# Zero products in the first softmax chain, running sums of squares over 73 tiles, and a sixth output buffer, in a fused attention and highway kernel

## The chip, the cores and the metric

The kernel runs on one core of a Trainium2 chip. The metric is the device time of one launch in microseconds (us), the median of several executions. The profile's span is counted from the first instruction and is 1.7 to 1.9 us shorter than the times. The engines are PE (TensorE, matrix products), DVE (VectorE), ACT (ScalarE), POOL (GpSimd, which here also issues the loads) and SP (SyncE, which issues the stores). The "granted clock" is the share of PE's full clock that the trace shows. In the trace of the kernel before it is full for 27.31 us from 14.29 on, half for 3.41 and full again for 228.69, which is 8, 1 and 67 times 3.41 us; pieces of that length, counted from where a trace's clock record starts, are called throttle windows here. The "issue" of a product is the time from its start to the next start when nothing is waited for.

## The reference

```python
# q, k, v: 4 batches x 6336 x 256 f32
qn = q / (np.linalg.norm(q, axis=1, keepdims=True) + 1e-06)
kn = k / (np.linalg.norm(k, axis=1, keepdims=True) + 1e-06)
s = kn.transpose(0, 2, 1) @ qn / tau          # 256 x 256 per batch
a = softmax(s, -1)
x = v @ a                                      # 6336 x 256 per batch
H = relu(x @ w_h); T = sigmoid(x @ w_t + b_t)  # highway layer
out = T * H + (1 - T) * x
```

Each batch has a reduction over all its rows (k'q and the norms), then a small chain of dependent steps (norms, softmax, transpose, products with the weights), and only then its outputs.

## The kernel before

Rows are cut into tiles of 128. Phase 1 of a batch takes one tile after another ("p1 tile"); the k'q product goes to `S`, the squared norms are the diagonals of k'k and q'q in `G`:

```python
for c in range(2):
    kc = kk[0:nr, bass.ts(c, P)]
    nc.tensor.matmul(S[:, c, :], kc, qq[0:nr, :], ...)      # 128x256
    nc.tensor.matmul(G[:, c, :], kc, kc, ...)               # 128x128
for c in range(2 if squared(b, j) is None else 0):
    qc = qq[0:nr, bass.ts(c, P)]
    nc.tensor.matmul(G[:, 2 + c, :], qc, qc, ...)           # 128x128
```

For some tiles ("squared" ones) ACT squares q and DVE adds the squares up, so PE is spared the last two products. A product with ones ("sums") then folds the sum over the partitions.

Outputs are made in 100 slots of two tiles. PE transposes v (`vt_bank`, four transposes to a slot, called a set here; DVE copies it to `vts`), then does three products: `zbank` (the gate, ACT takes the sigmoid to `tt`), `h` and `x`. DVE makes `th` and `ux`, POOL subtracts them into an output tile `o`. Between the slots of batch b, PE does the p1 tiles of batch b+1:

```python
for t in range(NSLOT):
    ...                                   # transposes of v, zbank, h, x
    pending.append((t, *products(t, h, x)))           # DVE: th, ux
    ...
    for _ in range(count):                            # p1 tiles of the next batch
        p1_tile(pb + 1, j); squares(pb + 1, j); done1 += 1
    if t not in (end1 - 1, end1):
        next_loads(2, now)                            # POOL issues loads
    room = DEFER - sum(t >= at for at in DRAIN)       # stores held back
    out_now = 0
    while len(stores) > room and out_now < 2:
        note(send_store(last), now); out_now += 1     # SP: 1 MB, four slots
```

So up to DEFER finished stores are kept waiting while loads are urgent, and at each slot listed in DRAIN one fewer is kept. How the transposes run ahead of the slots is a table (`TURNS`: at slot 61 two, at slot 68 none), and where each step of a chain goes is another.

Of the kernel before, what the change touches and what calls it, by code (L numbers as in the profile page):

```python
# [15 lines left out]
P = 128  # L16
# [3 lines left out]
def kernel(  # L20
# [41 lines left out]
    QFIRST = [QALL.index((b, 0)) for b in range(B)]  # L62
    QTILES = 8
    QRING = 6
    ORING = 5
    DEFER = 3
    DRAIN = [53, 74, 85]
    VG = [spans(6, 10, 12, 12, 9)] + [spans(12, 12, 12, 13)] * (B - 1)
    VTILES = 13
    VALL = [(b, g) for b in range(B) for g in range(len(VG[b]))]  # L70
# [1 line left out]
    VRING = 4  # L72
    NPAIR = (NS + 1) // 2
    LOOK = 3
    RAMP = 14
    REM_SLOT = 4
    START_US = 5

    CHAIN0 = (0, 0, 1, 2)
    HEAD = sum(CHAIN0)  # L80
    P1_END = [18, 42, 64]

    GATES = {9: 2, 24: 0, 28: 2, 57: 2, 60: 2, 61: 2, 62: 0, 68: 0, 70: 0, 73: 0, 95: 2}
    TURNS = {29: 0, 30: 2, 48: 1, 49: 2, 55: 2, 57: 2, 61: 2, 68: 0, 74: 0, 75: 0, 76: 0, 93: 2}
    VTS = 9
    TTS = 6

    PE_BIAS = (67, 70, 72, 74, 77)

    DVE_SUBS = (98, 99)  # L90

# [1 line left out]



    SQ_GROUPS = {1: (1, 4), 2: (2, 3, 4), 3: (3, 4)}
    SQ_TILES = 8
    SQ_CUTS = 4
    LULL = [0, 3, 1, 5]

    EARLY = {"sums": (0, "pre"), "norms": (0, "pre"), "invs": (2, "pre"), "cq": (2, "pe"), "logits": (3, "pre"), "exps": (3, "post"), "softmax": (4, "pre"), "at": (4, "pe"), "at_copy": (5, "pre"), "ahat": (5, "pe"), "ahat_copy": (6, "pre")}
    LAST = {"sums": (0, "pre"), "norms": (0, "pre"), "invs": (1, "pre"), "cq": (2, "pe"), "logits": (2, "post"), "exps": (4, "post"), "softmax": (4, "post"), "at": (6, "pe"), "at_copy": (8, "pre"), "ahat": (8, "pe"), "ahat_copy": (9, "pre")}
    PLACES = [None, EARLY, EARLY, LAST]

    ctx.enter_context(tc.manual_schedule())
    const_pool = ctx.enter_context(tc.tile_pool(name="consts", bufs=1))
# [44 lines left out]
    for n in range(QRING):  # L151
        load_q(n)
        load_k(n)
    bt_sb = const_pool.tile([65, C], f32, tag="bt")
    nc.vector.memset(bt_sb, 0.0)
    for r in (0, 32, 64):
        nc.sync.dma_start(out=bt_sb[r : r + 1, :], in_=moe_b_t.rearrange("(a m) -> a m", a=1))
# [19 lines left out]
    zeros = const_pool.tile([P, 2 * C], f16, tag="zeros")  # L177
    nc.vector.memset(zeros.bitcast(u16), 0)

    rem0 = const_pool.tile([P, 2, C], f16, tag="rem0")  # L180
    nc.vector.tensor_copy(out=rem0[0:REM, :, :], in_=rem0_32[0:REM, :, :])
    wht = const_pool.tile([P, 2, 2 * C], f16, tag="wht")

# [43 lines left out]
                used.add(("q", QFIRST[b] + g))  # L227


    sq_t, part_t, sum_t = {}, {}, {}  # L230
    cuts = []

    def squared(b, j):

        for n, g in enumerate(SQ_GROUPS.get(b, ())):
            s0, ns = QG[b][g]
            o = j - (s0 + ns - SQ_TILES)
            if 0 <= o < SQ_TILES:
                return n, g, o
        return None  # L240

    def squares(b, j):

        at = squared(b, j)
        if at is None or at[2] % 2 == 0:
            return
        n, g, o = at
        if o == 1:
            add_up(len(cuts) - SQ_CUTS)

            sq_t[b] = work_pool.tile(
                [P, SQ_TILES // 2, C, 2], f32, tag="sq", bufs=2, name=f"sq{b}_{n}"
            )
            if n == 0:
                count = len(SQ_GROUPS[b])
                part_t[b] = work_pool.tile(
                    [P, (count + 1) // 2, C, 2], f32, tag="sq_part", bufs=1, name=f"part{b}"
                )
                if count % 2:
                    nc.vector.memset(part_t[b][:, count // 2, :, 1], 0.0)  # L260
        q0 = j - 1 - QG[b][g][0]
        nc.scalar.activation(  # L262
            out=sq_t[b][:, o // 2, :, :].rearrange("p c u -> p u c"),
            in_=q_t[QFIRST[b] + g][:, q0 : q0 + 2, :], func=Act.Square,
        )
        if o == SQ_TILES - 1:
            sq, part = sq_t[b], part_t[b]
            for i in range(SQ_CUTS):
                cols = slice(i * C // SQ_CUTS, (i + 1) * C // SQ_CUTS)
                cuts.append((  # L270
                    part[:, n // 2, cols, n % 2],
                    sq[:, :, cols, :].rearrange("p m c u -> p c m u"),
                ))
            if n == len(SQ_GROUPS[b]) - 1:
                sum_t[b] = work_pool.tile([P, C], f32, tag="sq_sum", bufs=1, name=f"sum{b}")
                cuts.append((sum_t[b], part.rearrange("p m c u -> p c m u")))

    def add_up(k):
        while k > 0 and cuts:
            dst, source = cuts.pop(0)  # L280
            nc.vector.tensor_reduce(  # L281
                out=dst, in_=source, op=AluOp.add, axis=mybir.AxisListType.XY
            )
            k -= 1
# [4 lines left out]
    def chain(b):  # L289
# [105 lines left out]
        def exps():  # L395

            ar = st["ar"] = st["t1"]
            rs = st["rs"] = small("rs", [P, 2], bufs=2)
            for c in range(2):
                nc.scalar.activation(  # L400
                    out=ar[:, c, :], in_=st["t1"][:, c, :], func=Act.Exp,
                    scale=st["inv"][:, c : c + 1], accum_out=rs[:, c : c + 1],
                )
            if b == 0:
                preload_table(Act.Sigmoid)

                st["e16"] = small("e16", [P, 2, C], f16)
                for c in range(2):
                    nc.vector.tensor_copy(out=st["e16"][:, c, :], in_=ar[:, c, :])

# [301 lines left out]

    ones_hl = const_pool.tile([65, P], f16, tag="ones_hl")
    bt_hl = const_pool.tile([65, C], f16, tag="bt_hl")
    bt_r = const_pool.tile([65, C], f32, tag="bt_r")

    def bias_rows():
        nc.vector.memset(ones_hl.bitcast(u16), 0)
# [62 lines left out]
    next_loads(3, now)  # L781
    c0 = chain(0)

    def fill(n):
        nonlocal done1
        for _ in range(n):
            p1_tile(1, done1)
            done1 += 1

    c0["norms"]()  # L790
    c0["invs"]()
    fill(CHAIN0[0])
    c0["cq"]()
    c0["logits"]()
    turns = [(t, transpose(t)) for t in range(2)]
    fill(CHAIN0[1])
    c0["exps"]()
    c0["at"]()
    fill(CHAIN0[2])
# [21 lines left out]
    for t in range(NSLOT):  # L821
        b, i = divmod(t, NPAIR)
        ready = set(used)
        slot[0] = t
        run(t, "pre")
        zs = range(zdone, min(NSLOT, zdone + GATES.get(t, 1)))
        zdone = zs.stop
        turned = range(tdone, min(NSLOT, tdone + TURNS.get(t, 1)))
        tdone = turned.stop
        for s in zs:  # L830
            mains(s, zbank[s % 2], 2, True)
            gate_act(s, zbank[s % 2])
        if pending:
            last = subtract(*pending.pop())
        for s in turned[:1]:
            vt_copy(s, transpose(s))
        for s in zs:
            seed(s, zbank[s % 2])
        h = hx_tile(f"h{t}")
        mains(t, h, 1, False)  # L840
        x = hx_tile(f"x{t}")
        mains(t, x, 0, False)
        for s in turned[1:]:
            vt_copy(s, transpose(s))
        run(t, "pe")
        pending.append((t, *products(t, h, x)))
        add_up(2 if len(cuts) > SQ_CUTS else 1)
        run(t, "post")
        for s in turned:
            bb, ii = divmod(s, NPAIR)  # L850
            for g, (s0, ns) in enumerate(VG[bb]):
                if 2 * ii + 2 == s0 + ns or (g == len(VG[bb]) - 1 and ii == NPAIR - 1):
                    used.add(("v", VFIRST[bb] + g))
        if t == NSLOT - 1:
            last = subtract(*pending.pop())


        pb = done1 // (NS + 1)
        count = 0
        for s in turned:  # L860
            bb, ii = divmod(s, NPAIR)
            g = max(g for g in range(len(VG[bb])) if VG[bb][g][0] <= 2 * ii)
            now = max(now, landed.get((load_v, VFIRST[bb] + g), now))
        now += 1.5
        if pb < len(P1_END):
            left = P1_END[pb] - t
            if 0 <= t - end1 < len(LULL):
                due = LULL[t - end1]
            else:
                due = -(-((pb + 1) * (NS + 1) - done1) // left)  # L870
            for ahead in range(due):
                if left > 1 and tile_lands(done1 + ahead) > now + 0.43 * ahead:
                    break
                count += 1
        for _ in range(count):
            pb, j = divmod(done1, NS + 1)
            now = max(now, min(tile_lands(done1), now + 20.0)) + 0.43
            p1_tile(pb + 1, j)
            squares(pb + 1, j)
            done1 += 1  # L880
            if j == NS:
                end1 = t + 1
                steps = chain(pb + 1)
                for name, (at, when) in PLACES[pb + 1].items():
                    hooks.setdefault((t + 1 + at, when), []).append(steps[name])


        if t not in (end1 - 1, end1):
            next_loads(2, now)
        room = DEFER - sum(t >= at for at in DRAIN)  # L890
        out_now = 0
        while len(stores) > room and out_now < 2:
            note(send_store(last), now)
            out_now += 1
        vT_t.pop(t, None)
# [38 lines left out]
```

## Time and profile before

| | before |
|---|---|
| time, median | 279.58 us |
| span of the profile | 278.1 us |
| PE busy | 255.7 us (92%) |
| DVE busy | 200.5 us (72%) |
| HBM read / written | 78.4 MB / 26.0 MB |

PE's busy time is the first thing to read, but an average hides the stages: PE follows the loads up to 37.5 us, runs into the first chain until 48, and is then full to 266. The lines of these views stand in the prediction. A pair of numbers that the page does not give, the time at which a load landed, and the time at which PE first used it, I took from the trace, by pairing each load with the first product on its tiles. The execution that was traced took 279.9 us, a little more than the median. Holes of PE in the text are counted from the time at which it could have issued its next product; the views count them from the modelled end of the product before, which makes them about 0.16 us shorter (four zbank products that take 0.44 us of issue are shown as 0.60).

### The profile page before, as it was taken

How to read it: one execution, taken by the hardware profiler on the slowest of the kernel's cores; microseconds unless marked ns; L12 is line 12 of the kernel's file. 1: busy time of each engine (PE TensorE's matmuls, PEld its weight loads, DVE VectorE, ACT ScalarE, POOL GpSimd, SP SyncE). 2: the span in 40 equal slices, each digit the busy share in tenths (PEclk: the TensorE clock that was granted, in tenths of full speed). 3: DMA queues.
4: the chain of work that ended last, by engine and by line, in shares of the span. 5: the costliest groups of instructions: out<-in, count | busy, mean ns of one | idle time of the engine just before them, and what ended most of it. 6: DMA issues, size and time to landing. Idle time of an engine off the chain costs nothing.

```text
span 278.1 us, 6881 instructions
## 1 busy us (share of the span) xinstructions
PE 255.7 (92%) x2772; PEld 226.1 (81%) x2772; DVE 200.5 (72%) x436; ACT 159.1 (57%) x277; POOL 171.9 (62%) x191
## 2 busy tenths in 40 slices
PE   0689859999999899999999999999999999999990
PEld 0579757999999788899999988899998887999870
DVE  0060046994666885779999865678989999999993
ACT  1040055687264469588854677477753775777660
POOL 6232350899565393764689857464545797888780
PEclk9999997999999999999999999999999999999996
DMA  6999999999999999999999999999999877837353
GB/s 125 213 214 214 209 209 210 213 214 214 214 216 213 285 216 286 213 287 302 273 240 262 235 272 271 233 297 320 315 224 251 262 140 298 341 151 305 154 226 105
DMA packets 16726, 65.65 MB, mean 236 GB/s; under 512 B 1843, under 2 KB 4150, under 8 KB 13750
## 3 DMA queue, kind: packets, MB, share of 16 engines
q0 software_dynamic: 11744, 39.13, 71.1%
q1 hardware_dynamic: 4950, 26.09, 23.7%
q8 instruction: 21, 0.34, 0.5%
q14 instruction: 11, 0.09, 0.1%
HBM read 78.38 MB, written 25.95 MB: 375 GB/s over the span
## 4 chain that ended last, share of the span: by engine, by line
PE 81%; DMA 10%; DVE 5%; issue 1%; ACT 1%; POOL 0%; DVEq 0%; ACTq 0%; POOLq 0%
PE zbank L552 15%; PE h L552 15%; PE x L552 15%; PE S L217 13%; DMA k<-in_k_dram 10%; PE vt_bank L525 8%; PE G L220 6%; PE G L223 4%; PE ah L445 2%; DVE ux L625 1%; DVE th L620 1%; DVE vts L538 1%; PE sums L303 1%; DVE part L281 0%; ACT ssb L400 0%
## 5 line engine op out<-in xcount | busy, mean ns | idle before, releaser
L635 POOL TENSOR_TENSOR o<-th,ux 128x512 f32<-128x512 f32 x95 | 120.9, 1279 | 33.7 <-DVE ux L625 30.9
L552 PEld LDWEIGHTS <-vts 128*128 128x128 f16 x1200 | 109.7, 98 | 15.0 <-issue 4.2
L604 ACT ACTIVATE tt<-zbank 128x512 f32<-128x512 f32 x100 | 58.9, 596 | 63.5 <-PE zbank L552 56.4
L217 PE MATMUL S<-q,k 128*128 128x256 f16 x392 | 84.4, 278 | 10.3 <-DMA k<-in_k_dram 10.3
L220 PE MATMUL G<-k 128*128 128x128 f16 x392 | 75.2, 223 | 0.0
L620 DVE SCALAR_TENSOR_TENSOR th<-h,tt 128x512 f32<-128x512 f32 (+1 forms) x104 | 69.1, 667 | 5.4 <-PE h L552 1.0
L625 DVE SCALAR_TENSOR_TENSOR ux<-tt,x 128x512 f32<-128x512 f32 (+1 forms) x104 | 68.1, 657 | 0.0
L538 DVE COPY vts<-vt_bank 128x512 f16<-128x512 f16 x96 | 40.4, 421 | 29.0 <-PE vt_bank L525 28.8
L552 PE MATMUL x<-mr,vts 128*128 128x256 f16 (+1 forms) x400 | 60.5, 273 | 0.1
L552 PE MATMUL h<-mr,vts 128*128 128x256 f16 (+1 forms) x400 | 60.6, 273 | 0.0
L552 PE MATMUL zbank<-mr,vts 128*128 128x256 f16 (+1 forms) x400 | 59.5, 273 | 0.0
L608 ACT COPY zbank<-btb 128x512 f32<-128x512 f32 x93 | 54.5, 591 | 2.6
L217 PEld LDWEIGHTS <-k 128*128 128x128 f16 x392 | 39.1, 100 | 14.7 <-DMA k<-in_k_dram 10.7
L220 PEld LDWEIGHTS <-k 128*128 128x128 f16 x392 | 39.1, 100 | 0.9
L223 PE MATMUL G<-q 128*128 128x128 f16 x280 | 39.5, 224 | 0.0
L525 PE MATMUL vt_bank<-ident,v 128*128 128x128 f16 x392 | 38.1, 219 | 0.6 <-DVE vts L538 0.4
L525 PEld LDWEIGHTS <-v 128*128 128x128 f16 x392 | 29.8, 98 | 4.1 <-issue 1.9
L123 POOL DMA_DIRECT2D q<-in_q_dram x28 | 15.8, 563 | 20.8 <-DMA q<-in_q_dram 7.0
L129 POOL DMA_DIRECT2D k<-in_k_dram x28 | 15.3, 546 | 21.5 <-DMA k<-in_k_dram 10.4
L223 PEld LDWEIGHTS <-q 128*128 128x128 f16 x280 | 22.2, 100 | 2.0
L281 DVE TENSOR_REDUCE part<-sq 128x64 f32<-128x512 f32 x28 | 18.7, 682 | 0.0
L262 ACT ACTIVATE sq<-q 128x512 f32<-128x512 f16 x28 | 18.5, 674 | 0.0
(99 smaller groups left out, 112.3 us busy)
## 6 DMA issues: line engine op xcount, KB each, us to landing
out_dram<-o SPq DMA_DIRECT2D x23, 1024.0 KB, 9.0
q<-in_q_dram POOLq DMA_DIRECT2D x20, 512.0 KB, 18.4
k<-in_k_dram POOLq DMA_DIRECT2D x20, 512.0 KB, 19.9
v<-in_v_dram POOLq DMA_DIRECT2D x11, 768.0 KB, 22.0
v<-in_v_dram POOLq DMA_DIRECT2D x3, 832.0 KB, 28.0
out_dram<-o SPq DMA_DIRECT2D x4, 256.0 KB, 2.0
q<-in_q_dram POOLq DMA_DIRECT2D x3, 320.0 KB, 18.1
k<-in_k_dram POOLq DMA_DIRECT2D x3, 320.0 KB, 17.2
```

The lines of the kernel that those rows point to most:

```text
L217: nc.tensor.matmul(S[:, c, :], kc, qq[0:nr, :], start=first and c == 0, stop=last and c == 1)
L220: nc.tensor.matmul(G[:, c, :], kc, kc, start=first and c == 0, stop=False)
L223: nc.tensor.matmul(G[:, 2 + c, :], qc, qc, start=False, stop=last and c == 1)
L281: nc.vector.tensor_reduce(out=dst, in_=source, op=AluOp.add, axis=mybir.AxisListType.XY)
L525: nc.tensor.transpose(ps[:, u, c, 0 : nr[u]], vt[0 : nr[u], bass.ts(c, P)], ident[0 : nr[u], 0 : nr[u]],)
L538: nc.vector.tensor_copy(out=sb, in_=ps)
L552: nc.tensor.matmul(dst[0:r, u, :], vT_t[t][:, u, kt, 0:r], mr[:, part, kt, :], start=(not seeded and kt == 0 and (u == 0 or i == NPAIR - 1 ...
L604: nc.scalar.activation(out=tt_t[s], in_=z, func=Act.Sigmoid)
L608: nc.scalar.copy(out=z, in_=btb)
L620: nc.vector.scalar_tensor_tensor(out=th[pr, us, :], in0=h[pr, us, :], scalar=0.0, in1=tt[pr, us, :], op0=AluOp.max, op1=AluOp.mult,)
L625: nc.vector.scalar_tensor_tensor(out=ux[pr, us, :], in0=tt[pr, us, :], scalar=1.0, in1=x[pr, us, :], op0=AluOp.subtract, op1=AluOp.mult,)
L635: last = eng.tensor_tensor(out=ot[pr, o0 + us.start : o0 + us.stop, :], in0=th[pr, us, :], in1=ux[pr, us, :], op=AluOp.subtract,)
```

## The change

The intent: keep PE's clock up in the first chain with products of zeros; let ACT and DVE square 73 tiles instead of 56, in runs that need not follow the load groups, with the sum carried from one run into the next instead of being kept in parts; and hold one more store back, which takes a sixth output buffer. The tables of placements are retuned with it. Its core:

```diff
-    ORING = 5
-    DEFER = 3
-    DRAIN = [53, 74, 85]
+    ORING = 6
+    DEFER = 4
+    DRAIN = [56, 75, 72, 79]
+    WARM = (14, 9)
-    CHAIN0 = (0, 0, 1, 2)
+    CHAIN0 = (0, 0, 0, 4)
-    TURNS = {29: 0, 30: 2, 48: 1, 49: 2, 55: 2, 57: 2, 61: 2, 68: 0, 74: 0, 75: 0, 76: 0, 93: 2}
+    TURNS = {49: 2, 51: 1, 52: 2, 59: 1, 61: 2, 64: 0, 72: 0, 73: 0, 93: 2}
-    SQ_GROUPS = {1: (1, 4), 2: (2, 3, 4), 3: (3, 4)}
+    SQ_RUNS = {1: (6, 14, 21, 28), 2: (17, 26, 35), 3: (13, 22, 32)}
...
+        for i in range(SQ_CUTS):
+            cuts.append((
+                sq_t[b][:, SQ_TILES // 2 - 1, cols, 1] if more else sum_t[b][:, cols],
+                sq[:, :, cols, :].rearrange("p m c u -> p c m u"),
+            ))
...
+    def keep_warm(n):
+        bank = hx_tile("warm")
+        for i in range(n):
+            nc.tensor.matmul(bank[:, i % 2, :], zeros[:, 0:P], zeros[:, 0:C], ...)
...
     c0["invs"]()
+    keep_warm(WARM[0])
...
     fill(CHAIN0[1])
+    keep_warm(WARM[1])
     c0["exps"]()
```

Cut: the tables of gates, bias slots and chain steps, the constants by which loads and p1 tiles are spread over the slots, the code of the runs, and some constants that moved into shared buffers to make room.

More of the change, by code (lines that the diff above doesn't have):

```diff
@@ L74 @@
     LOOK = 3
-    RAMP = 14
-    REM_SLOT = 4
-    START_US = 5
-    CHAIN0 = (0, 0, 1, 2)
+    RAMP = 11
+    REM_SLOT = 3
+    START_US = 4
+    WARM = (14, 9)
+    CHAIN0 = (0, 0, 0, 4)
     HEAD = sum(CHAIN0)
     P1_END = [18, 42, 64]
-    GATES = {9: 2, 24: 0, 28: 2, 57: 2, 60: 2, 61: 2, 62: 0, 68: 0, 70: 0, 73: 0, 95: 2}
-    TURNS = {29: 0, 30: 2, 48: 1, 49: 2, 55: 2, 57: 2, 61: 2, 68: 0, 74: 0, 75: 0, 76: 0, 93: 2}
+    GATES = {14: 2, 20: 0, 24: 2, 51: 2, 54: 2, 55: 2, 58: 0, 67: 0, 69: 0, 73: 0, 95: 2}
+    TURNS = {49: 2, 51: 1, 52: 2, 59: 1, 61: 2, 64: 0, 72: 0, 73: 0, 93: 2}
     VTS = 9
     TTS = 6
-    PE_BIAS = (67, 70, 72, 74, 77)
+    PE_BIAS = (71, 72, 76, 79, 97)
     DVE_SUBS = (98, 99)
     V_HELD = {}
-    SQ_GROUPS = {1: (1, 4), 2: (2, 3, 4), 3: (3, 4)}
+    SQ_RUNS = {1: (6, 14, 21, 28), 2: (17, 26, 35), 3: (13, 22, 32)}
     SQ_TILES = 8
     SQ_CUTS = 4
-    LULL = [0, 3, 1, 5]
-    EARLY = {"sums": (0, "pre"), "norms": (0, "pre"), "invs": (2, "pre"), "cq": (2, "pe"), "logits": (3, "pre"), "exps": (3, "post"), "softmax": (4, "pre"), "at": (4, "pe"), "at_copy": (5, "pre"), "ahat": (5, "pe"), "ahat_copy": (6, "pre")}
-    LAST = {"sums": (0, "pre"), "norms": (0, "pre"), "invs": (1, "pre"), "cq": (2, "pe"), "logits": (2, "post"), "exps": (4, "post"), "softmax": (4, "post"), "at": (6, "pe"), "at_copy": (8, "pre"), "ahat": (8, "pe"), "ahat_copy": (9, "pre")}
-    PLACES = [None, EARLY, EARLY, LAST]
+    SQ_RATE = 2
+    LULL = [2, 3, 0, 4]
+    EARLY = {"sums": (0, "pre"), "norms": (0, "pre"), "invs": (1, "pre"), "cq": (1, "pe"), "logits": (2, "pre"), "exps": (2, "post"), "softmax": (4, "pre"), "at": (4, "pe"), "at_copy": (5, "pre"), "ahat": (5, "pe"), "ahat_copy": (6, "pre")}
+    MID = {"sums": (0, "pre"), "norms": (0, "pre"), "invs": (2, "pre"), "cq": (2, "pe"), "logits": (2, "post"), "exps": (3, "post"), "softmax": (3, "post"), "at": (5, "pe"), "at_copy": (6, "pre"), "ahat": (6, "pe"), "ahat_copy": (7, "pre")}
+    LAST = {"sums": (0, "pre"), "norms": (0, "pre"), "invs": (2, "pre"), "cq": (2, "pe"), "logits": (2, "post"), "exps": (3, "pre"), "softmax": (5, "post"), "at": (7, "pe"), "at_copy": (8, "pre"), "ahat": (8, "pe"), "ahat_copy": (9, "pre")}
+    PLACES = [None, EARLY, MID, LAST]
     ctx.enter_context(tc.manual_schedule())
@@ L153 @@
         load_k(n)
-    bt_sb = const_pool.tile([65, C], f32, tag="bt")
+    bt_sb = work_pool.tile([P, 2, C], f32, tag="ux", bufs=4, name="bt_sb")[0:65, 0, :]
     nc.vector.memset(bt_sb, 0.0)
@@ L178 @@
     nc.vector.memset(zeros.bitcast(u16), 0)
-    rem0 = const_pool.tile([P, 2, C], f16, tag="rem0")
+    rem0 = work_pool.tile([P, 2, 2, P], f16, tag="vTs", bufs=VTS, name="rem0").rearrange(
+        "p u c r -> p u (c r)"
+    )
     nc.vector.tensor_copy(out=rem0[0:REM, :, :], in_=rem0_32[0:REM, :, :])
@@ L227, in p1_tile, with q_tiles @@
                 used.add(("q", QFIRST[b] + g))
-    sq_t, part_t, sum_t = {}, {}, {}
+    sq_t, sum_t = {}, {}
     cuts = []
     def squared(b, j):
-        for n, g in enumerate(SQ_GROUPS.get(b, ())):
-            s0, ns = QG[b][g]
-            o = j - (s0 + ns - SQ_TILES)
-            if 0 <= o < SQ_TILES:
-                return n, g, o
-        return None
+        for n, j0 in enumerate(SQ_RUNS.get(b, ())):
+            count = SQ_TILES - (n > 0)
+            if j0 <= j < j0 + count:
+                return n, j - j0, count
+        return None
+    def q_tiles(b, j, count):
+        g = max(i for i in range(len(QG[b])) if QG[b][i][0] <= j)
+        o = j - QG[b][g][0]
+        return q_t[QFIRST[b] + g][:, o : min(o + count, QG[b][g][1]), :]
     def squares(b, j):
         at = squared(b, j)
-        if at is None or at[2] % 2 == 0:
+        if at is None:
             return
-        n, g, o = at
-        if o == 1:
-            add_up(len(cuts) - SQ_CUTS)
+        n, o, count = at
+        if o == 0 and n == 0:
             sq_t[b] = work_pool.tile(
@@ L253, in squares @@
             )
-            if n == 0:
-                count = len(SQ_GROUPS[b])
-                part_t[b] = work_pool.tile(
-                    [P, (count + 1) // 2, C, 2], f32, tag="sq_part", bufs=1, name=f"part{b}"
-                )
-                if count % 2:
-                    nc.vector.memset(part_t[b][:, count // 2, :, 1], 0.0)
-        q0 = j - 1 - QG[b][g][0]
-        nc.scalar.activation(
-            out=sq_t[b][:, o // 2, :, :].rearrange("p c u -> p u c"),
-            in_=q_t[QFIRST[b] + g][:, q0 : q0 + 2, :], func=Act.Square,
-        )
-        if o == SQ_TILES - 1:
-            sq, part = sq_t[b], part_t[b]
-            for i in range(SQ_CUTS):
-                cols = slice(i * C // SQ_CUTS, (i + 1) * C // SQ_CUTS)
-                cuts.append((
-                    part[:, n // 2, cols, n % 2],
-                    sq[:, :, cols, :].rearrange("p m c u -> p c m u"),
-                ))
-            if n == len(SQ_GROUPS[b]) - 1:
-                sum_t[b] = work_pool.tile([P, C], f32, tag="sq_sum", bufs=1, name=f"sum{b}")
-                cuts.append((sum_t[b], part.rearrange("p m c u -> p c m u")))
+        sq = sq_t[b]
+        if o % 2 == 0 and o < count - 1:
+            return
+        first = o - o % 2
+        while first <= o:
+            src = q_tiles(b, j - o + first, o + 1 - first)
+            u = first % 2
+            nc.scalar.activation(
+                out=sq[:, o // 2, :, u : u + src.shape[1]].rearrange("p c u -> p u c"),
+                in_=src, func=Act.Square,
+            )
+            first += src.shape[1]
+        if o < count - 1:
+            return
+        add_up(len(cuts))
+        more = n < len(SQ_RUNS[b]) - 1
+        if more:
+            sq_t[b] = work_pool.tile(
+                [P, SQ_TILES // 2, C, 2], f32, tag="sq", bufs=2, name=f"sq{b}_{n + 1}"
+            )
+        else:
+            sum_t[b] = work_pool.tile([P, C], f32, tag="sq_sum", bufs=1, name=f"sum{b}")
+        for i in range(SQ_CUTS):
+            cols = slice(i * C // SQ_CUTS, (i + 1) * C // SQ_CUTS)
+            cuts.append((
+                sq_t[b][:, SQ_TILES // 2 - 1, cols, 1] if more else sum_t[b][:, cols],
+                sq[:, :, cols, :].rearrange("p m c u -> p c m u"),
+            ))
     def add_up(k):
@@ L405, in exps @@
                 preload_table(Act.Sigmoid)
-                st["e16"] = small("e16", [P, 2, C], f16)
+                st["e16"] = work_pool.tile(
+                    [P, 2, 2, P], f16, tag="vTs", bufs=VTS, name="e16"
+                ).rearrange("p u c r -> p u (c r)")
                 for c in range(2):
@@ L714 @@
     bt_hl = const_pool.tile([65, C], f16, tag="bt_hl")
-    bt_r = const_pool.tile([65, C], f32, tag="bt_r")
+    bt_r = work_pool.tile([P, 2, C], f32, tag="ux", bufs=4, name="bt_r")[0:65, 0, :]
     def bias_rows():
@@ L782 @@
     c0 = chain(0)
+    def keep_warm(n):
+        bank = hx_tile("warm")
+        for i in range(n):
+            nc.tensor.matmul(
+                bank[:, i % 2, :], zeros[:, 0:P], zeros[:, 0:C], start=True, stop=True,
+                skip_group_check=True,
+            )
     def fill(n):
@@ L846 @@
         pending.append((t, *products(t, h, x)))
-        add_up(2 if len(cuts) > SQ_CUTS else 1)
+        add_up(2 if len(cuts) > SQ_RATE else 1)
         run(t, "post")
```

## The prediction

> **What bounds the kernel now.** I read first which engine is busy in each stage, then what that engine waits for, then its clock, then the order of instructions in the one stage where it is not busy. The stretches (busy time of each engine, then granted clock, DMA share, GB/s):
>
> ```profile
> core 0: us, PE busy (x) PEld busy (x) DVE busy (x) ACT busy (x) POOL busy (x), PEclk, DMA share, GB/s
> 9.50:37.50 28.00, 26.10 (x304) 23.00 (x302) 4.63 (x22) 3.37 (x7) 8.07 (x16) 1.00 1.09 211
> 37.50:48.00 10.50, 7.02 (x60) 5.53 (x61) 6.75 (x28) 6.66 (x15) 2.77 (x5) 0.84 1.13 212
> 48.00:92.00 44.00, 44.00 (x507) 40.57 (x505) 32.07 (x59) 26.13 (x45) 32.82 (x38) 1.00 1.06 218
> 92.00:154.00 62.00, 61.26 (x682) 54.66 (x679) 52.67 (x108) 41.86 (x72) 40.88 (x46) 1.00 1.05 261
> 154.00:213.00 59.00, 58.99 (x664) 52.75 (x662) 45.75 (x97) 38.33 (x67) 35.73 (x36) 1.00 1.04 269
> 213.00:266.00 53.00, 52.76 (x528) 45.75 (x526) 51.04 (x111) 38.88 (x68) 42.22 (x37) 1.00 0.67 231
> ```
>
> Up to 37.5 us PE follows the loads of batch 0. From 37.5 to 48 (the first softmax chain) it is busy 7.02 of 10.5 us, at a mean clock of 0.84. From 48 to 266 PE has no holes but two: 0.74 us after 92 and 0.24 in the last stretch. So time there falls only if PE gets less to do, or nothing at all happens. DVE is close behind from 213 on (51.04 of 53). The DMA engines are full up to about 203 us, but PE does not wait for them after 37.5, as its list of waits shows (total, times, longest):
>
> ```profile
> PE S L217 <- DMA k<-in_k_dram: 10.3, 2, 9.2
> PE cq L372 <- DVE dcat L350: 1.7, 1, 1.7
> PE at L435 <- DVE e L409: 1.3, 2, 1.1
> ...
> PE sums L303 <- DVE sum L281: 0.7, 1, 0.7
> ```
>
> The two data waits of L217 are in the load stage. The wait for "sums" is the hole after 92: the last tile of batch 1 ends at about 94.0, DVE still adds up squares (two reductions and the sum over partial sums), and the product starts at 94.78.
>
> The clock, in pieces of one throttle window (the trace's granted clock falls to half at 41.60 and comes back at 45.01, 3.41 us later):
>
> ```profile
> 26.60:30.00 3.40, 2.34 (x33) 2.05 (x31) 0.00 (x0) 0.00 (x0) 0.71 (x1) 1.00 1.06 210
> 34.80:38.20 3.40, 2.70 (x37) 2.39 (x34) 0.66 (x7) 0.70 (x2) 1.70 (x4) 1.00 1.23 201
> 38.20:41.60 3.40, 1.30 (x14) 1.09 (x14) 2.37 (x14) 2.88 (x9) 2.00 (x4) 1.00 1.12 220
> 41.60:45.00 3.40, 3.22 (x20) 2.37 (x19) 2.12 (x7) 2.00 (x4) 0.14 (x1) 0.50 1.05 216
> ```
>
> The window with PE busy 1.30 of 3.40 us (38%) is followed by one at half clock. Windows with 2.34 (69%) and 2.70 (79%) are not. In the slow one lie the transposes of the attention matrix, one tile of batch 1 and the "ah" products, that is the chain itself:
>
> ```profile
> 41.95 0.40 PE L435 MATMUL at<-ident,e 128*128 128x128 f16 x2 [0.18 <-DVE e L409]
> 42.14 0.42 PE L217 MATMUL S<-q,k 128*128 128x256 f16 x1
> 42.38 0.42 DVE L441 COPY at_sb<-at 128x512 f16<-128x512 f16 x1 [0.49 <-PE at L435]
> 42.99 1.92 PE L445 MATMUL ah<-wht,at_sb 128*128 128x256 f16 x8
> 44.94 0.47 ACT L468 ACTIVATE mr<-ah,rinv 128x256 f16<-128x256 f32 x1 [0.38 <-PE ah L445]
> 45.45 0.48 DVE L470 TENSOR_SCALAR mr<-ah,rinv 128x256 f16<-128x256 f32 x1 [0.78 <-ACT mr L468]
> 45.85 0.41 DVE L538 COPY vts<-vt_bank 128x512 f16<-128x512 f16 x1
> 46.32 0.38 PE L525 MATMUL vt_bank<-ident,v 128*128 128x128 f16 x4 [0.42 <-DVE vts L538]
> ...
> 48.75 0.60 PE L552 MATMUL zbank<-mr,vts 128*128 128x256 f16 x4
> ```
>
> PE's next work after its tiles (the transposes at 46.32) waits for a DVE copy, which waits for a DVE scaling, which waits for ScalarE, which waits for the slow "ah" products.
>
> [...] 3.41 us at half clock, and 0.21 us instead of 0.109 from one 256-column matmul to the next. [...] the median step of G<-q here is 56 ns. [...] the trace has 682 ns for 512 elements (60 ns less when the next follows at once, as 0.60 us steps show). [...] here PE is already full after 48 us, so only the first 48 us and PE's own work have anything to give.
>
> **The change part by part.**
>
> *Zero products.* 14 products (128x256) go after the first norms, 9 after the first transposes of v. At 0.109 us: 14 x 0.109 = 1.53 us, from 37.4 to 38.9, and the chain's cq starts at 39.21; 9 x 0.109 = 0.98 us, from about 40.2 to 41.2, and the transposes start at 41.46. Both fit into the holes with 0.25 us to spare. They take a bank of the three-bank ring each time, and by the order of allocation none is awaited. The window from 38.2 gets 0.7 + 0.98 us more, so 1.30 becomes 3.0 of 3.40 (88%), above the 69% that kept the clock. I take it that the clock stays full.
>
> *What that and the new order give in the chain.* One tile of batch 1 stood before "ah", two behind it and a fourth in slot 0; now four stand behind. The copy of the transposed matrix ends 0.1 us sooner (42.7); "ah" takes 8 x 0.109 = 0.87, to 43.6; four tiles at 0.44 (36.01 to 36.45, from one to the next) end at 45.4. The other branch: last "ah" result about 43.8, ScalarE to 44.4, DVE to 44.9, copy to 45.3, so it no longer holds PE. The transposes start at 45.4 instead of 46.32. From them to the zbank product of slot 1 it was 48.75 - 46.32 = 2.43 us, less the tile that has moved (0.44) 1.99, so that product starts at 47.4: **1.35 us** gained.
>
> *Squares.* 73 tiles instead of 56 (29 instead of 16 in batch 1, 22 for 24 in batch 2, 22 for 16 in batch 3). Each takes two 128x128 products from PE: 17 x 2 x 0.056 = **1.9 us**, all where PE is full. ScalarE gets 31 pairs and 11 single tiles for 28 pairs: 3 x 0.674 + 11 x about 0.48 (like the 128x256 exponentials, 0.50) = +7.3 us, of 63.5 that it idles before tt. DVE gets 40 reductions of 0.682 for 28 plus three sums and a memset: 27.3 for 22.0, +5.3 us. Batch 1 is densest: six squared tiles a slot, so PE 1.53 + 6 x 0.33 = 3.5 us, ScalarE about 1.15 + 3 x 0.64 = 3.1, DVE 1.53 + 2.4 = 3.9 in two slots that flush four reductions and 2.7 in the next. DVE falls back 0.9 us and recovers, with two slots of copies in hand. I count nothing for it.
>
> *The sum carried along.* The partial sums and their last reduction (0.69) go. Behind the last tile of batch 1 DVE has two reductions (1.2 us) instead of two and the sum (1.9). The hole before "sums" shrinks from 0.8 to 0.15: **0.65 us**.
>
> *Sixth buffer, later drains.* A store waits for a fifth finished group instead of a fourth, so at least 1 MB of stores, at 2.5 us each (the step between 1 MB loads, as 70.3, 72.8, 75.4 us), is behind the loads until slot 72. No wait is removed by it today; it makes room for the faster PE.
>
> *Rest.* Five bias products by PE stay five; one moves to slot 97, in the tail, where it replaces a ScalarE copy that PE waited 0.13 us for. Pace in the tail stays 1.53 us a slot: zero.
>
> Sum: 1.35 + 1.9 + 0.65 = 3.9 us, so 275.7. Two tenths of small stalls make it **275.8 us** (-1.35%).
>
> **The rivals.**
>
> *The loads become the bound.* Against landing times, first uses have 4 to 6 us to spare in batch 1, but 3.8 for the sixth group of batch 2, 0.9 for the sixth of batch 3 (landed 196.5, used 197.4) and 0.8 for the last v group of batch 2 (206.7, 207.5). PE comes there about 3.7 us sooner. One deferred store gives 2.5, two (between slots 53 and 56) give 5. So the wait would be 3.7 - 0.9 - 2.5 = 0.3 us at worst by this sum. If stores were not what delays these loads, it would be 2.8 us, and the time 278.5. The 90% and more of DMA share to 203 us speaks against that[...].
>
> *The clock drops in spite of the zeros* [...]. Then 0.85 us of "ah" and the cold tiles come back, some 1.2 us: 277.0. For it: the idle gap around the copy at 42.4 remains. Against it: 69% was enough.
>
> *DVE or ScalarE becomes the bound* in batch 1 or in the chain of batch 3 (DVE 96% there). Half of the 1.9 us would be lost: 276.8. Against it: at 213 on, DVE has one reduction of 0.6 in place of the sum's 0.69, nothing more.
>
> *Much more than predicted.* PE has only 1.0 us of holes after 48 us, so beyond 4.3 us nothing is left: 275.3. 2% would be 274.0.
>
> **Range and chances.** Centre 275.8; the upper side takes one rival of about 1.3 us, the lower side the holes: 274.9 to 277.3. Faster by over 2% needs 5.6 us, more than PE's holes and removed work hold: 0.03. Slower by over 2% needs several rivals at once: 0.01.
>
> **What would show it.** Right: granted clock 1.0 through the first chain, "ah" pace 0.109, the zbank product of slot 1 near 47.4; G<-q down from 280 to 246; the wait of "sums" gone; PE full from 48 us on, last PE work about 4 us sooner; the tail from slot 64 as long as before. Wrong: a half-clock window before 48 us; PE waits for k, q or v after 160 us; PE waits for vts or tt between slots 11 and 18; a longer last stretch.

The paces were read from the trace of the kernel before: 0.109 us from one 256-column product to the next, 0.056 from one 128-column product to the next, 0.682 for one reduction.

## The result, and the profile after

The changed kernel took 277.56 us (276.77 to 277.79, 4 runs) against 279.54 for the kernel before in the same rounds. The ratio is 0.9925 (95% interval 0.9902 to 0.9947). Such a ratio is the mean time of one kernel's fast runs over that of the other's of the same rounds, so it is not quite the ratio of the quoted medians. The prediction said 275.8, with a range from 274.9 to 277.3: the direction was right, the gain was 2.0 us instead of 3.7, and the time lies outside the range.

The stretches of the changed kernel, columns as before (busy time and instructions of PE, PEld, DVE, ACT, POOL; granted clock; DMA share; GB/s):

```profile
core 0: us, PE busy (x) PEld busy (x) DVE busy (x) ACT busy (x) POOL busy (x), PEclk, DMA share, GB/s
37.50:48.00 10.50, 9.49 (x101) 7.83 (x98) 7.61 (x30) 7.09 (x15) 2.88 (x5) 1.00 1.15 213
154.00:213.00 59.00, 57.63 (x638) 51.33 (x636) 46.54 (x97) 40.54 (x73) 35.27 (x36) 1.00 1.05 272
213.00:266.00 53.00, 52.60 (x528) 45.74 (x527) 51.60 (x105) 38.57 (x68) 42.83 (x37) 1.00 0.69 240
```

The first chain is what was forecast: the clock is 1.00 and PE is busy 9.49 us of 10.5, the zeros included. But 154 to 213, which had 58.99 of 59 before, now has 57.63. PE's waits (total, times, longest; lines cut) name it:

```profile
PE vt_bank L543 <- DMA v<-in_v_dram: 1.4, 1, 1.4
...
PE cq L393 <- ACT dcat L374: 0.3, 1, 0.3
PE x L570 <- DVE th L638: 0.3, 1, 0.3
```

A wait of 1.4 us for a load of v is new; so are 0.3 us before the last chain's cq and 0.3 us before one x. In order of time, around slot 61 of the changed kernel (start, duration, engine, line):

```profile
204.25 0.60 PE L570 MATMUL zbank<-mr,vts 128*128 128x256 f16 x4
206.21 0.40 PE L543 MATMUL vt_bank<-ident,v 128*128 128x128 f16 x4 [1.36 <-DMA v<-in_v_dram]
206.44 0.38 PE L570 MATMUL h<-mr,vts 128*128 128x256 f16 x2
```

Four zbank products take 0.44 us of issue, so the transposes could have begun at 204.69; they began at 206.21, 1.52 us later, when the last v group of batch 2 had landed. The chain that ended last, in order of time, therefore runs through that load for 31.78 us:

```profile
174.38 31.78 DMA v<-in_v_dram
```

Where the gain stood at each slot (start of the slot's first h product, us):

| | before | changed | gained so far |
|---|---|---|---|
| slot 1 | 49.41 | 48.04 | 1.37 |
| slot 18 (batch 1 summed) | 95.88 | 92.28 | 3.60 |
| slot 42 (batch 2 summed) | 155.27 | 152.31 | 2.96 |
| slot 61 | 206.65 | 202.26 | 4.39 |
| slot 62 | 208.85 | 206.44 | 2.41 |
| slot 64 (batch 3 summed) | 214.56 | 211.71 | 2.85 |
| slot 94 | 262.63 | 260.43 | 2.20 |
| end of the span | 278.1 | 276.0 | 2.1 |

So the gain had been made, and was given back: at slot 61 to 62, and again between 64 and 94. (The smaller fall from slot 18 to 42 is a hole of 0.4 us at 130.7, and two squared tiles fewer than before in batch 2.)

The work that was to move did move. The groups of the page, PE's q'q products (280 before) and ACT's squares (28 before):

```profile
L230 PE MATMUL G<-q 128*128 128x128 f16 x246 | 34.2, 221 | 0.0
...
L272 ACT ACTIVATE sq<-q 128x512 f32<-128x512 f16 (+1 forms) x42 | 23.8, 606 | 0.0
```

### The profile page after: what moved, and what is told of

Its sections match the earlier page's. It is cut to its first block, busy times and chain, and to the rows that moved or that the text cites. A ratio compares the mean times of both kernels' runs of the same rounds, so it can differ in the third digit from the quotient of the medians.

```text
span 276.0 us, 6880 instructions
## 1 busy us (share of the span) xinstructions
PE 254.0 (92%) x2761; PEld 224.9 (81%) x2761; DVE 204.4 (74%) x444; ACT 164.3 (60%) x291; POOL 172.0 (62%) x191
## 4 chain that ended last, share of the span: by engine, by line
PE 69%; DMA 21%; DVE 5%; issue 1%; ACT 1%; POOL 1%; DVEq 0%; ACTq 0%; POOLq 0%
PE x L570 13%; PE h L570 13%; PE zbank L570 13%; DMA v<-in_v_dram 12%; PE S L224 11%; DMA k<-in_k_dram 10%; PE vt_bank L543 7%; PE G L227 5%; PE G L230 3%; PE ah L463 1%; DVE ux L643 1%; DVE th L638 1%; DVE vts L556 1%; PE sums L319 1%; PE cq L393 1%
## 5 line engine op out<-in xcount | busy, mean ns | idle before, releaser
L224 PE MATMUL S<-q,k 128*128 128x256 f16 x392 | 81.8, 276 | 10.4 <-DMA k<-in_k_dram 10.4
L227 PE MATMUL G<-k 128*128 128x128 f16 x392 | 73.6, 221 | 0.0
L230 PE MATMUL G<-q 128*128 128x128 f16 x246 | 34.2, 221 | 0.0
L272 ACT ACTIVATE sq<-q 128x512 f32<-128x512 f16 (+1 forms) x42 | 23.8, 606 | 0.0
L230 PEld LDWEIGHTS <-q 128*128 128x128 f16 x246 | 19.3, 99 | 1.6
L297 DVE TENSOR_REDUCE sq<-sq 128x64 f32<-128x512 f32 x28 | 18.0, 677 | 0.0
```

Source lines behind the costliest of these rows:

```text
L224: nc.tensor.matmul(S[:, c, :], kc, qq[0:nr, :], start=first and c == 0, stop=last and c == 1)
L227: nc.tensor.matmul(G[:, c, :], kc, kc, start=first and c == 0, stop=False)
L230: nc.tensor.matmul(G[:, 2 + c, :], qc, qc, start=False, stop=last and c == 1)
L272: nc.scalar.activation(out=sq[:, o // 2, :, u : u + src.shape[1]].rearrange("p c u -> p u c"), in_=src, func=Act.Square,)
```

## The experiments

My theory after the result: the loads took the gain. PE reached the last v group of batch 2 sooner, but that load landed almost when it did before (206.2 against 206.7), because two stores of 1 MB each are let go just before it. Rivals: the wait only hides another limit (POOL, DVE, the last stretch); or the landing is set by when the load is issued; or the added squares cost more than was counted. Each run below was done in several rounds with the kernel before on the same chip (medians 279.41 to 279.65); runs of different groups were on two chips.

### Later release of the stores

```diff
-    DRAIN = [56, 75, 72, 79]
+    DRAIN = [62, 75, 72, 79]
```

The traces show the same order of instructions on all five engines as in the changed kernel; only the times differ.

> The changed kernel with one number altered: the first of the four points at which held-back stores are let go, slot 56, becomes slot 62, so one 1 MB store fewer runs before the last v group of batch 2 lands. My theory (the loads took the gain: PE stood 1.4 to 1.5 us at slot 61 for that v group, landed 206.2): it lands about 2.5 us sooner, the wait of PE for v goes from 1.4 to under 0.3 us, the time falls by 1.2 to 1.5 us, from 277.5 to 276.0 to 276.4. Rival 1 (the wait only hides another limit: GpSimd's lag, VectorE, k27 or the last stretch): the wait goes but the time stays within 0.4 us of 277.5. Rival 2 (the landing is set by when the load is issued, not by the stores): the v group still lands near 206 and nothing changes.

Measured: 276.36 us (276.34 to 276.68, 5 runs), ratio to before 0.9883 (0.9865 to 0.9901). That is 1.1 to 1.2 us less than the changed kernel. The same transposes, which now follow the zbank products of 204.15 at once:

```profile
204.59 0.39 PE L543 MATMUL vt_bank<-ident,v 128*128 128x128 f16 x4
```

The v group landed at 201.9 instead of 206.2. The stores show why. SP's issues in the kernel before, then in the changed one, then in this one (each line is one store of 1 MB):

```profile
187.68 0.33 SPq L590 DMA_DIRECT2D out_dram<-o  x1
```

```profile
189.87 0.33 SPq L590 DMA_DIRECT2D out_dram<-o  x1
```

```profile
192.36 0.33 SPq L608 DMA_DIRECT2D out_dram<-o  x1
```

```profile
196.77 0.33 SPq L608 DMA_DIRECT2D out_dram<-o  x1
```

```profile
206.46 0.33 SPq L608 DMA_DIRECT2D out_dram<-o  x1
```

The store at 187.68 is the eleventh and the one at 189.87 the twelfth of the kernel before. In the changed kernel the eleventh goes at 192.36 and the twelfth at 196.77, so at 206 both kernels have sent the same twelve large stores, and the changed one has sent its last two closer to the load. Only two small stores (192 KB together) are still held back there that the kernel before had sent at 200.30. In this run the eleventh goes at 196.66 and the twelfth at 206.46, after the landing. Rival 2 (set by the issue) falls: the load was issued at 174.3, as before, and landed 4.3 us sooner. Rival 1 falls for this wait: the time went with it. The load came 4.3 us sooner where 2.5 was expected; why is not shown.

### Without the zeros, with both settings of the stores

```diff
-    WARM = (14, 9)
+    WARM = (0, 0)
```

(`keep_warm` then takes no bank either.)

> The changed kernel without the 23 products of zeros. Both theories: half clock for one window of 3.41 us around 41.6 to 45.0, and the product that opens slot 1 comes 0.9 to 1.4 us later than 47.4. My theory (PE then waits for the v group whose landing the DMA sets, near 206.2): PE's wait for v shrinks by the same amount, so at the end only 0 to 0.4 us are lost: 277.5 to 277.9. Rival (what the zeros save reaches the end): 278.5 to 278.9.

> Late drain as in e1 and no zeros as in e2. My theory: with the v wait gone, the zeros are worth their full 0.9 to 1.4 us: this is slower than e1 by that much, 277.0 to 277.6. Rival (zeros are worth nothing because something else later binds in any case): the same as e1 within 0.3 us.

Measured: 278.09 us (277.27 to 278.91, 6 runs) with the stores of the change, and 278.05 (277.59 to 278.47, 6 runs) with the later release. So the zeros are worth about 0.6 us in the changed kernel (against 277.48 to 277.56; the intervals of the ratios, 0.9920 to 0.9962 and 0.9901 to 0.9947, overlap) and 1.7 us once the v wait is gone (against 276.36; 0.9924 to 0.9957 and 0.9865 to 0.9901, clear of each other). The same cause is worth more when the load does not take it back. Both numbers are a little above what I expected (0 to 0.4, and 0.9 to 1.4). The record has a likely reason: the executions without zeros fall in two groups, 277.27 to 278.09 us at a mean clock of 0.986 to 0.988 and 278.32 to 278.91 at 0.981 to 0.982. The step of 0.006 is that of one more window at half clock (3.41 us at half of it are 0.006 of the span). Only the first group was traced.

The wait for v did not shrink as I expected, either: in the traced run with the stores of the change it is gone, because the load landed at 203.70, not at 206.2, and PE came to it at 205.70. The same two stores went there at 193.38 and 197.78, 1.0 us later than in the changed kernel. That run was the fastest of its six, so it does not speak for the others, but it suggests that the landing follows the times of the stores and not only their number.

The first product of slot 1 comes at 48.81 instead of 47.38 without zeros, 1.43 us later. The clock, in two throttle windows of the run without zeros (with the stores of the change; same columns as above):

```profile
38.98:42.39 3.41, 1.73 (x16) 1.20 (x16) 2.08 (x9) 3.16 (x7) 1.32 (x3) 1.00 1.10 220
42.39:45.79 3.40, 3.14 (x18) 2.39 (x19) 2.31 (x8) 1.52 (x4) 0.00 (x0) 0.50 1.25 205
```

and in the changed kernel, whose windows lie elsewhere:

```profile
36.60:40.01 3.41, 3.31 (x37) 2.83 (x35) 2.06 (x15) 2.22 (x4) 1.77 (x3) 1.00 1.22 215
40.01:43.43 3.42, 2.58 (x27) 1.81 (x24) 2.35 (x8) 2.89 (x9) 1.11 (x2) 1.00 1.08 201
```

PE busy 1.73 of 3.41 us is followed by half clock; 3.31 and 2.58, zeros included, are not. The edit is the zeros alone: with these 23 products the clock stayed at 1.00, without them it was 0.50 for one window. What share of busy time it takes is not shown, and the share of the profile does not sort the windows: busy 1.68 of 3.41 (36.63 to 40.04, without zeros and with the late release) was followed by a window at 1.00, and 1.73 was not.

### Five buffers again

```diff
-    ORING = 6
-    DEFER = 4
-    DRAIN = [56, 75, 72, 79]
+    ORING = 5
+    DEFER = 3
+    DRAIN = [53, 74, 85]
```

> The changed kernel with the store settings of the kernel before: five output buffers, three held-back stores, let go at slots 53, 74, 85. My theory: one store more (1 MB, 2.5 us) runs before the loads of batch 3, so the sixth q and k groups of batch 3 (slack 1.2 us now) and the last v group (0 now) keep PE waiting 2 us more: 278.5 to 280. Rival (the sixth buffer does nothing, stores do not delay loads): 277.5 within 0.4.

Measured: 278.46 us (278.38 to 278.71, 6 runs). So about one microsecond of the changed kernel's gain goes with the store settings. The loads of batch 3 did land later (the sixth k group at 196.6, not 193.4). But the edit is not one of stores alone: the builder places loads by its own estimate of the DMA, and the trace shows POOL's loads and subtractions in another order from 116 us on. And the wait was not where I put it: the sixth k group of batch 3 kept PE for 0.3 us, and the v group had landed as PE came to it. The larger hole, 1.6 us, lay at 140.3, before an x product that waited for DVE (1.4 us in the list of waits). It is the same kind of hole as the one at 130.7 in the changed kernel, which a later run takes up. How much of the microsecond is due to the stores and how much to POOL's order was not separated.

### Fewer squares

```diff
-    SQ_RUNS = {1: (6, 14, 21, 28), 2: (17, 26, 35), 3: (13, 22, 32)}
+    SQ_RUNS = {1: (6, 14), 2: (17, 26, 35), 3: (13, 22)}
```

> The late-drain kernel (e1, 276.4 us) with three runs of squares left out, 21 of the 73 tiles, so PE does their 42 products of 128 columns itself. My theory (squares are worth PE's time, 2 x 0.056 us a tile, where nothing else waits): 42 x 0.056 = 2.35 us more, 278.5 to 278.8. Rival (ScalarE's and VectorE's added work took part of it, so leaving it out gives part back): at most 277.5.

This one, as the next two, is built on the late release. Measured: 278.65 us (278.17 to 278.75, 6 runs), 2.29 us more than 276.36; 42 x 0.056 = 2.35 was expected. So these squares are worth what PE is spared; ACT's and DVE's added work cost nothing that shows.

### The last chain's reciprocals one slot sooner

```diff
-    LAST = {..., "invs": (2, "pre"), ...}
+    LAST = {..., "invs": (1, "pre"), ...}
```

> The late-drain kernel with the reciprocals of the last chain placed one slot sooner (slot 65 instead of 66), as in the kernel before. My theory (PE's 0.48 us before the last cq comes from VectorE doing the reciprocal too late, and PE is the bound of the last stretch): the hole goes, 0.3 to 0.5 us less, 275.9 to 276.1. Rival (the last stretch is VectorE's): no change within 0.2 of 276.4, the hole turns up elsewhere.

Measured: 276.44 us (276.30 to 276.51, 4 runs). My theory fell and the rival held: the hole of 0.48 us before cq is gone from the trace, and holes of 0.22 and 0.43 us stand before two sets of transposes that wait for DVE's copies. That fits DVE as the bound from slot 64 on; the runs with other turns below test it from the other side.

### Loads issued later in POOL's order

```diff
-    SLACK = 4.0
+    SLACK = 2.0
```

In the changed kernel POOL stood 4.40 us in front of one k load. The lines of POOL, DVE and PE around it:

```profile
128.62 0.53 POOL L134 DMA_DIRECT2D k<-in_k_dram  x1 [4.40 <-PE vt_bank L543]
130.49 0.69 DVE L638 SCALAR_TENSOR_TENSOR th<-h,tt 128x512 f32<-128x512 f32 x1 [1.02 <-POOL o L653]
131.23 0.60 PE L570 MATMUL x<-mr,vts 128*128 128x256 f16 x4 [0.25 <-DVE th L638]
```

POOL's subtractions came late, DVE waited 1.02 us for a buffer that they free, PE then waited for DVE. The profile names a product of PE as what POOL waited for; that had long been done. The q load that was eight loads earlier landed at 128.1, just before POOL went on, so I take it that the load waited for its semaphore to be free. The packed trace fits this: the two loads are signalled on the same semaphore, and each of the three loads before went 0.4 to 0.6 us after the landing of the load eight before it. No run varied the number of semaphores.

> The late-drain kernel with GpSimd issuing loads somewhat later in its order (the lead allowed to a load over its lane's landing goes from 4 to 2 us). My theory (GpSimd stood 4.4 us in front of one k load near 124, its subtractions came late, VectorE waited 1.0 us for a buffer and PE 0.4): the wait before x goes, 0.3 to 0.4 us less, 276.0. Rival (loads issued later land later): PE waits for k or v after 160 us, 276.5 to 277.5.

Measured: 276.23 us (276.01 to 276.32, 4 runs). The hole before x is gone. The time fell by 0.1 to 0.2 us, less than half of the hole: the sixth k group of batch 3 now lands 0.4 us before its use instead of 1.2, and that stretch is at its margin. The intervals of the ratios (0.9862 to 0.9896, and 0.9865 to 0.9901 without this edit) overlap, so it is a small gain at most.

### Zeros alone in the kernel before

```diff
     c0["norms"]()
     c0["invs"]()
+    keep_warm(14)
     fill(CHAIN0[0])
...
     fill(CHAIN0[1])
+    keep_warm(9)
     c0["exps"]()
```

> The kernel before with only the zero products added (14 and 9, at the same places), old order of tiles, five buffers. The clock should stay full in the first chain. My theory: the product that opens slot 1 comes 0.8 to 1.1 us sooner than 48.75, but the loads of batch 3 have only 0.8 to 0.9 us to spare, so 0.6 to 0.9 us reach the end: 278.6 to 278.9. Rival 1 (all of it and more reaches the end): 278.2 or less. Rival 2 (loads eat it): 279.3 or more.

Measured: 279.44 us (279.22 to 280.71, 6 runs) against 279.41 for the kernel before in the same rounds; ratio 1.001 (0.9988 to 1.0032). Rival 2 held, by the times: the first product of slot 1 came at 47.66 instead of 48.75, 1.09 us sooner, and nothing of it reached the end that the times can tell (the interval leaves room for 0.3 us at most). The two traces alone say less: their spans, 277.5 and 278.1, still differ by 0.6 us, but the traced execution of the kernel before was one of its slower ones (279.9). In the trace PE now waits for the sixth k group of batch 3, at the first line below, whose predecessor began at 196.43:

```profile
196.81 0.28 PE L217 MATMUL S<-q,k 128*128 128x256 f16 x1 [0.16 <-DMA k<-in_k_dram]
```

Without a store held longer, that k group and the last v group meet PE with 0.0 and 0.2 us to spare. The kernel before itself agrees in part: two of its executions, in the rounds of the first four experiments, had a mean granted clock of 0.996 and 0.997, which leaves no room for a half-clock window in the chain (3.41 us at half of it cost 0.006 of the mean), and they took 279.38 and 279.49 us, as those at 0.988 to 0.991 (279.18 to 279.66). But its four executions at 0.983 to 0.985 took 279.78 to 280.48, and two of the six with zeros took 280.55 and 280.71; what slowed these is not known.

### Control, and the last stretch

> The changed kernel once more, unaltered, as a control on this chip. Both theories: 277.4 to 277.8, with the last v group of batch 2 waited for by 1 us or more; if single runs differ, by that wait.

The changed kernel again: 277.48 us (276.99 to 277.91, 6 runs), ratio 0.9916. Its profiled run, the slowest, had 2.3 us of hole before the same transposes and took 277.91. The wait is a property of the kernel. Why it was longer here, the two traces show:

```profile
206.31 0.40 PE L543 MATMUL vt_bank<-ident,v 128*128 128x128 f16 x4 [2.14 <-DMA v<-in_v_dram]
```

The load landed at 206.26 here and at 206.16 there, but PE came to slot 61 at 201.58 instead of 202.26. The 0.7 us by which this execution was ahead were all lost at this load: slot 62 starts at 206.54 and 206.44.

> Late drain, later issues and the early reciprocals of the last chain together. If VectorE is the bound of the last stretch: as later issues alone (276.2), within 0.15. If PE is: 0.3 to 0.5 less.

Later release, later issues and early reciprocals together: 276.14 us (276.02 to 276.38, 4 runs), as later issues alone (276.23) within 0.1, which is what the theory of a last stretch bound by DVE forecast.

```diff
-    TURNS = {49: 2, 51: 1, 52: 2, 59: 1, 61: 2, 64: 0, 72: 0, 73: 0, 93: 2}
+    TURNS = {49: 2, 51: 1, 52: 2, 59: 1, 61: 2, 63: 2, 68: 0, 74: 0, 75: 0, 76: 0, 93: 2}
```

> Late drain and later issues, and the transposes of v done ahead as the kernel before did them: one more at slot 63, and the slots that skip one are 68, 74, 75, 76 instead of 64, 72, 73. Two of VectorE's copies (0.42 us, 0.33 net of overlap) move from the last stretch to before slot 64. My theory (the last stretch is VectorE's, 98% busy with 30 copies where the kernel before had 28): 0.5 to 0.8 us less than 276.2, so 275.4 to 275.7. Rival (PE's holes of 0.5 and its own work set the last stretch; the transposes only move): 276.2 within 0.15.

> As the last, with the reciprocals of the last chain one slot sooner as well. With two copies fewer VectorE is less the bound and PE's hole before the last cq may count: 0 to 0.4 us less than the last. The fastest of all that I have: 275.2 to 275.6.

From the first th of slot 64 to that of slot 94, the instructions that touch `vts` (PE, PEld, DVE), in the kernel before, the changed one and the one with this edit:

```profile
215.30:263.80 48.50, 44.42 (x354) 32.72 (x353) 11.19 (x28) 1.00 0.69 238
```

```profile
212.40:261.60 49.20, 44.77 (x355) 32.78 (x353) 12.02 (x30) 1.00 0.73 254
```

```profile
211.10:259.60 48.50, 44.27 (x354) 32.70 (x352) 11.20 (x29) 1.00 0.76 268
```

DVE copies 28, 30 and 28 sets (the 29th of the last line began before slot 64), and the stretch lasts 48.50, 49.15 and 48.52 us. The edit with the turns took 275.96 us (275.93 to 276.10, 4 runs), and with the reciprocals as well 275.80 (275.51 to 275.99, 4 runs), ratio to before 0.9856 (0.9838 to 0.9874). The stretch gave 0.64 us as the theory says (two copies, 0.33 net each; PE's part of what moved, two sets of 0.22 us, would give 0.44). But only 0.2 to 0.3 reached the end, below the 0.5 to 0.8 expected. (The pair from the same rounds is the three together against all four: 276.14 and 275.80, runs that do not overlap, though the intervals of their ratios, 0.9857 to 0.9888 and 0.9838 to 0.9874, do.) Slot 63 became 0.45 us longer (3.30 instead of 2.85 from its h to the next), since PE's transposes moved there with the copies. The version with all four edits beats both kernels: 3.8 us (1.4%) less than before, 1.7 us less than the changed one.

| kernel | median us | runs |
|---|---|---|
| before | 279.41 to 279.65 | 4 to 11 a group |
| changed | 277.56, again 277.48 | 4, 6 |
| late release | 276.36 | 5 |
| no zeros | 278.09 | 6 |
| late release, no zeros | 278.05 | 6 |
| five buffers | 278.46 | 6 |
| late release, 52 squared tiles | 278.65 | 6 |
| late release, early reciprocals | 276.44 | 4 |
| late release, later issues | 276.23 | 4 |
| the three together | 276.14 | 4 |
| late release, later issues, turns | 275.96 | 4 |
| all four | 275.80 | 4 |
| before, with zeros | 279.44 | 6 |

## Why the prediction was wrong

**The first chain: right.** It foresaw full clock, zeros that fit their holes with 0.25 us to spare (0.26 and 0.27 in the trace), and the first product of slot 1 at 47.4; that came at 47.38. The clock from 37.5 to 48 was 1.00, where the kernel before had 0.84.

**The squares and the sum carried along: right.** PE's q'q products fell by 34, the wait for the first "sums" is gone, and taking 21 tiles out again cost 2.29 us of 2.35. At slot 61, before any wait for v, the gain was 4.39 us. Of that 0.66 is no gain but work put off: the changed tables have done one set of gate products (4 x 0.109 us) and one set of transposes (4 x 0.056 us) fewer by then. The remaining 3.73 is close to the forecast sum of 3.9, with 0.4 lost at 130.7. (Two small readings of the prediction are off and change nothing: reductions that follow at once step by 0.60 us, 80 ns less than one takes and not 60; and the loads of batch 1 have 1.2 us to spare in the first k group and 4.2 to 6.7 in the others, not 4 to 6.)

**The sixth buffer and the loads: the step that failed.** The prediction said that at least 1 MB of stores stays "behind the loads until slot 72", and the first rival, that "One deferred store gives 2.5, two (between slots 53 and 56) give 5. So the wait would be 3.7 - 0.9 - 2.5 = 0.3 us at worst". It counted the places in the queue of stores, not which stores they were. At the last v group, one of the held places is the 192 KB of a batch's end, and twelve large stores have gone in both kernels; the release at slot 56 and the one at slot 58 put two of them at 192.36 and 196.77. The load landed 0.5 us sooner, not 2.5. PE came to its first use 2.8 us sooner (204.69 instead of 207.52; it was 4.4 us ahead at slot 61, but the changed table of turns asks for this group at slot 62 and no longer at 61) and had 0.8 to spare. In the terms of the prediction, 3.7 - 0.9 - 2.5 = 0.3 became 2.8 - 0.8 - 0.5 = 1.5 us of waiting (2.3 in the control). The term that failed is the 2.5: the new store settings were worth 0.5 us to this load. The rival was the right one and was given the wrong size, from the k group, where one more store did make room (193.4 instead of 196.5). That stores issued by SP delay a load issued by POOL, the late release shows: sending two of 1 MB later, by 4.3 and 9.7 us (the second after the landing), moved the landing from 206.2 to 201.9.

**"Pace in the tail stays": wrong by 0.65 us.** The prediction took the last stretch as unchanged because each slot is. But the changed table of turns leaves two more copies to DVE there, 30 instead of 28, and DVE is busy 48.1 of 49.2 us. The prediction had the line that shows DVE at 51.04 of 53 and drew on it only for a rival in batch 1 and the last chain, where it counted "one reduction of 0.6 in place of the sum's 0.69, nothing more" and not the copies. Moving the two copies back shortens the stretch by 0.64 us, and 0.2 to 0.3 of it reaches the end.

**Not foreseen: POOL's place in the order.** The loads' waits hold POOL's subtractions behind them (4.40 us in front of one k load, after which DVE waited 1.02 us for a buffer). This cost PE 0.4 us once in the changed kernel, and 1.6 us with five buffers. Its removal gave 0.1 to 0.2 us, within the noise.

**The range.** It allowed for one rival of 1.3 us above the sum. One rival of 1.2 us (by the late release) and a lengthened tail came together. With the release, the issues, the turns and the reciprocals mended, the kernel takes 275.80 us (275.51 to 275.99): the number that was predicted for a kernel in which nothing waits. That they meet so closely is partly luck, since the later issues were no part of the prediction.

What stays open: why the landing moves by 4.3 us when the two stores go later, and by 2.5 us when they go only 1.0 us later, where 2.5 us was the step between loads; and why the slower executions are slow.

## What to carry to other kernels

When an engine is full, ask of each thing that it will reach sooner how much time it has to spare there, and compare that with the whole gain made up to that point; work saved before a load that cannot come sooner is lost, as the control's lead of 0.7 us was. Ask of a held-back store whether it is let go before the load lands or after: here the last v group landed at 206.2 with two stores let go at 192.36 and 196.77, and at 201.9 with the same two at 196.66 and 206.46. So list which stores go when, not how many are held. And a retuned table that moves work from a stage with room to one without it lengthens that stage though nothing was added, here to 49.15 us with 30 copies from 48.50 with 28.
